# Attention of an attention-and-experts kernel, from eight batches of 128-token chunks to sixteen steps on 64x64 tiles

## The chip, the cores and the metric

The kernel runs on one core of one Trainium2 chip. The metric is the device time of one execution in microseconds (us), the median of three runs. A core has a matrix engine (PE, with its weight loads shown as PEld), three engines for elementwise work (DVE, ACT, POOL), and a queue engine SP that issues most DMAs. Matmuls read SBUF and write PSUM; both have 128 partitions.

## The reference, cut to what matters

```python
kv  = np.einsum('bhsd,bhse->bhde', k, v)      # b = 8 batches, h = 8 heads, s = 576, d = e = 64
out = np.einsum('bhsd,bhde->bhse', q, kv)
rms = np.sqrt(np.mean(out * out, axis=-1, keepdims=True) + 1e-06)
x   = (out / rms * g_norm)                    # then heads side by side: x[b, s, 512]
logits     = x @ w_gate                       # 8 experts
local_gate = sigmoid(x @ w_local)
# token by token in a batch: e = argmax(logits) if s == 0 or local_gate < 0.5,
# otherwise the expert of the token before
out[b, s] = softmax(logits)[e] * (relu(x @ w1[e]) @ w2[e])   # w1 512x1024, w2 1024x512
```

All arrays are float32.

## The kernel before, in words

The program has two parts. The first does the attention, the gate logits and the routing; the second runs the experts over tokens sorted by expert, with weights split into a high and a low half (`wsplit`) so that three fast matmuls stand for one of full precision.

**Attention.** The loop goes over the 8 batches. `load(b)` fetches k, v and q of one batch: of each head the first (or, for odd heads in k and v, the last) 512 tokens as four tokens to a partition on 128 partitions, and the 64 tokens that are left over two heads to a tile. `stage_kv` makes kv of all heads in the PSUM tile `pk`: 4 matmuls over 128 tokens and one over 64, for each head, two heads side by side on the columns of the array (L365). `stage_t` transposes kv and `stage_m` multiplies it by the gate weights, so that the logits come out of the same matmul as the output: the block matrix `kvb` holds kv and these gate columns. `stage_q` transposes q on PE into `pq`, and ACT copies it to `qT`. `out_two` then multiplies `qT` by `kvb`, two tokens and 146 columns at a time, on the whole array (L455), and `out_last` does the left-over tokens on 64x64 tiles (L471). ACT copies the result from `po` to `raw`. `squares` and a DVE sum give the mean square of each head, `rows_out` the normalisation and gate values, and `store` writes the rows of a batch to the DRAM array `xs`. After each pair of batches `route` works out, with a few matmuls into `rbank`, which expert each token takes and its place among that expert's tokens.

**Order.** The work of one batch is written down in pieces (`prepare`, `chunks`), and `step` puts pieces of `rows_out` and `route` between them with high priority. The order on PE, ACT, DVE and POOL in this part is then made by the planner of the language, from its own estimate of times. DMAs of SP run in the order in which they are written. k and v, and q, have two buffers of one batch each.

**Hand-over.** `begin` gathers the first two blocks of 128 tokens of expert 0 out of `xs`, splits that expert's weights, and turns the tokens; the first expert matmuls are in `first_wide` (written `ph`, L846). A third block follows when three quarters of the stores have landed, a fourth when all have. The rest of the second part has an order written by hand already and is the same in both kernels.

Of the kernel before, what the change touches and what calls it, by code (L numbers as in the profile page):

```python
# [22 lines left out]
def kernel(  # L23
# [22 lines left out]
    KS = 4  # L46
    PR = S - KS * P
    C = 2 * KS + 1
    KD = KS * D
# [3 lines left out]
    HB = 2 * PW  # L53
    KW = NG + HW + HB
    XO = NG
    NGRP = B // 2
    NCH = NGRP * C

# [11 lines left out]
    NM = NP * C // 2  # L70
# [54 lines left out]

    left = ctx.enter_context(ExitStack())
# [5 lines left out]
    lq = work.enter_context(tc.tile_pool(name="lq", bufs=2, reuse_waits="tile"))  # L132
# [10 lines left out]
    ld = right.enter_context(tc.tile_pool(name="ld", bufs=2, side="right", reuse_waits="tile"))  # L143
# [6 lines left out]
    ps_o = ps1.enter_context(tc.tile_pool(name="ps_o", bufs=4, space=PSUM,  # L150
# [71 lines left out]
    def heads(t):  # L222
        return t[:, 0:H * KD].rearrange("p (h c) -> p h c", h=H)

    def rest(t):
        return t[:, H * KD:].rearrange("p (n d) -> p n d", n=NP)

    def load(b):
        kt = ld.tile([P, H * KD + NP * D], F32, name="kt")
        vt = ld.tile([P, H * KD + NP * D], F32, name="vt")  # L230
        qt = lq.tile([P, H * KD + NP * D], F32, name="qt")
# [6 lines left out]
        kv = (k, kt), (v, vt)  # L238
        for src, dst in kv:
            main(dst, src, slice(0, H, 2), 0)  # L240
        for src, dst in kv:
            fetch(rest(dst), src[b].rearrange("(n x) s d -> n (x s) d", x=2)[
                :, KS * P:KS * P + P].rearrange("n p d -> p n d"))
        for src, dst in kv:
            main(dst, src, slice(1, H, 2), PR)
        if b >= 4:
            store(b - 4)
        main(qt, q, slice(0, H), 0)
        for y in range(2):
            fetch(rest(qt)[y * PR:(y + 1) * PR],  # L250
                  q[b, y * NP:(y + 1) * NP, KS * P:].rearrange("h p d -> p h d"))
        if b == B - 1:
            for i in range(NW1):
                wload(0, i)
        return kt, vt, qt

    loads = {b: load(b) for b in range(2)}
# [11 lines left out]


    FAR = 64
    cs = rc.tile([P, C], F32, name="cs")
# [3 lines left out]
    id1 = rc.tile([P, NGRP, C], F32, name="id1")  # L276

    def iota(dst, pattern, base, mult=0):
        nc.gpsimd.iota(dst, pattern=pattern, base=base, channel_multiplier=mult,
                       allow_small_or_imprecise_dtypes=True)  # L280

    for bb in range(2):
        js = slice(bb * (KS + 1), bb * (KS + 1) + KS)
        iota(cs[:, js], [[1, KS]], 2 * FAR * bb)
        iota(s8[:, js], [[E, KS]], 0, E * KS)
        iota(id1[:, :, js], [[2 * S, NGRP], [1, KS]], bb * S + 1, KS)
        nc.gpsimd.memset(m0[0:1, js.start:js.start + 1], 1.0)
        rows = slice(bb * PR, (bb + 1) * PR)
        iota(s8[rows, KS:KS + 1], [[E, 1]], E * KS * P, E)
        iota(id1[rows, :, KS:KS + 1], [[2 * S, NGRP], [1, 1]], bb * S + KS * P + 1, 1)  # L290
    nc.gpsimd.memset(cs[:, KS:KS + 1], float(FAR))
    m11 = rc.tile([P, C, C], F32, name="m11")
    csd = wk.tile([P, C, C], F32, name="csd", bufs=1)
    nc.vector.tensor_sub(csd, cs.unsqueeze(2).to_broadcast([P, C, C]),
# [58 lines left out]
    def stage_kv(b):  # L353
# [4 lines left out]
        if not b:  # L358
            order.sort(key=lambda x: x[2])
# [448 lines left out]
    for kvb in prepare(0):  # L808
        pass
# [419 lines left out]
```

## Time and profile before

| what | value |
|---|---|
| median of 3 runs | 620.85 us (619.88 to 621.93) |
| profiled execution | 623.8 us |
| its span, first to last instruction | 622.1 us |
| mean granted PE clock | 0.979 |
| PE, DVE, ACT, POOL busy | 588.8, 299.4, 232.9, 113.9 us |
| moved by DMA | 94.10 MB, 151 GB/s in the mean |
| first expert matmul | 140.18 us from the span's start |

A busy PE is not PE at its peak: matmuls are pipelined, and their records overlap. A row of a group gives its line, engine, operation, tiles (out<-in), shapes and count, then the union of its busy time in us, the mean duration of one in ns, and the engine's idle time just before them with what ended it. [...]

### The profile page before, as it was taken

The page shows a single profiled execution, that of the slowest core. Times are in us where ns is not written, and L with a number is a line of the kernel's source. Part 1 is how long each engine was busy: PE and PEld are TensorE (multiplying, and loading weights), DVE is VectorE, ACT ScalarE, POOL GpSimd, SP SyncE. Part 2 cuts the span into 40 slices and gives each one's busy share as a digit, 9 for nine tenths or more (in the row PEclk, how much of TensorE's full clock was granted, in tenths as well). Part 3 has the DMA queues.
Part 4 walks back from the last instruction along what each step waited for, and adds up shares of the span by engine and source line. Part 5 has one row for each costly group of instructions (what it writes and reads, how often), then busy time and mean ns, then how long its engine had stood idle before and what let it go on. Part 6 is the DMA issues. An engine that isn't in the chain of part 4 may idle for free. (4 is left out here: it accounts for less than half of the span.)

```text
span 622.1 us, 10287 instructions
## 1 busy us (share of the span) xinstructions
PE 588.8 (95%) x4069; PEld 519.3 (83%) x4069; DVE 299.4 (48%) x703; ACT 232.9 (37%) x392; POOL 113.9 (18%) x144
## 2 busy tenths in 40 slices
PE   5899998989897799999999999999999999999996
PEld 4788887878675798989897989899888979897895
DVE  2177988796736343615343436254525444362410
ACT  0266564484125323323333333234333333333310
POOL 5022313200152003011121120113020211201001
PEclk9999999878999799999999999999999999999999
DMA  9999999949376324323153323344342525231000
GB/s 249 278 310 301 299 259 280 307 164 279 124 245 215 107 77 140 103 101 116 68 174 103 109 82 110 136 119 139 103 141 79 174 98 154 75 114 58 1 35 23
DMA packets 63864, 94.10 MB, mean 151 GB/s; under 512 B 17471, under 2 KB 42047, under 8 KB 63808
## 3 DMA queue, kind: packets, MB, share of 16 engines
q1 hardware_dynamic: 56192, 72.31, 39.0%
q0 software_dynamic: 6304, 21.04, 10.9%
q8 instruction: 34, 0.56, 0.4%
q10 hardware_dynamic: 1312, 0.02, 0.1%
q14 instruction: 22, 0.18, 0.1%
HBM read 73.48 MB, written 20.53 MB: 151 GB/s over the span
## 5 line engine op out<-in xcount | busy, mean ns | idle before, releaser
L886 DVE SCALAR_TENSOR_TENSOR hl<-ph,hh 128x384 fp32r<-128x384 f32 (+3 forms) x92 | 53.4, 580 | 148.7 <-ACT hh L885 120.9
L880 POOL DMA_INDIRECT out_dram<-ot,sidr x36 | 35.4, 984 | 343.3 <-ACT ot L879 343.3
L885 ACT ACTIVATE hh<-ph 128x384 fp32r<-128x384 f32 (+3 forms) x92 | 46.9, 509 | 131.8 <-PE ph L852 126.4
L879 ACT ACTIVATE ot<-py,pe 128x512 f32<-128x512 f32 (+2 forms) x37 | 25.4, 687 | 111.7 <-issue 57.7
L365 PE MATMUL pk<-vt,kt 128*64 128x64 f32 (+1 forms) x640 | 42.7, 245 | 7.4 <-DMA vt<-in_v_dram 7.1
L365 PEld LDWEIGHTS pk<-vt,kt 128*64 128x64 f32 (+1 forms) x640 | 33.6, 146 | 16.9 <-issue 10.9
L744 POOL DMA_INDIRECT xr<-xs,gidr x36 | 37.8, 1051 | 24.7 <-DVE gs L1106 8.0
L455 PE MATMUL po<-kvb,qT 128*128 128x146 f32 x256 | 39.5, 300 | 0.0
L455 PEld LDWEIGHTS po<-kvb,qT 128*128 128x128 f32 x256 | 35.2, 198 | 0.8
L771 DVE SCALAR_TENSOR_TENSOR yl<-pt,gcol,yh 128x512 fp32r<-128x512 f32 x20 | 15.0, 751 | 37.0 <-ACT yh L770 36.8
L444 POOL TENSOR_TENSOR sq<-raw 128x512 f32<-128x512 f32 x17 | 17.7, 1044 | 74.1 <-ACT raw L457 38.6
L383 PE MATMUL pq<-ident,qt 128*128 128x128 f32 x128 | 24.1, 328 | 3.4 <-DVE kvb L415 2.8
L457 ACT COPY raw<-po 128x438 f32<-128x438 f32 (+1 forms) x48 | 22.5, 481 | 13.0 <-PE po L455 12.9
L385 ACT COPY qT<-pq 128x512 f32<-128x512 f32 x32 | 18.4, 585 | 19.4 <-PE pq L383 17.0
L445 DVE TENSOR_REDUCE ms<-sq 128x8 f32<-128x512 f32 x36 | 23.7, 680 | 3.6 <-ACT sq L442 2.7
L757 DVE TENSOR_TENSOR xr<-xr 128x512 f32<-128x512 f32 x37 | 25.3, 684 | 0.0
L846 PE MATMUL py<-w_1h,hh 128*128 128x512 f32 (+2 forms) x58 | 23.4, 403 | 0.0
L846 PE MATMUL py<-w_0h,hh 128*128 128x512 f32 (+2 forms) x58 | 23.3, 401 | 0.0
L766 PEld LDWEIGHTS pt<-ident,xr 128*128 128x128 f32 x148 | 18.3, 141 | 5.6 <-DVE xl L771 0.6
L852 PE MATMUL py<-w_0h,hl 128*128 128x512 f32 (+2 forms) x58 | 22.9, 394 | 0.1
L851 PE MATMUL py<-w_0l,hh 128*128 128x512 f32 (+2 forms) x58 | 22.8, 392 | 0.0
L852 PE MATMUL py<-w_1h,hl 128*128 128x512 f32 (+2 forms) x58 | 22.7, 392 | 0.0
(364 smaller groups left out, 1658.1 us busy)
## 6 DMA issues: line engine op xcount, KB each, us to landing
wst<-in_moe_w_dram SPq DMA_DIRECT2D x64, 512.0 KB
xs<-raw SPq DMA_DIRECT2D x8, 1132.0 KB
kt<-in_k_dram SPq DMA_DIRECT2D x16, 512.0 KB
vt<-in_v_dram SPq DMA_DIRECT2D x16, 512.0 KB
qt<-in_q_dram SPq DMA_DIRECT2D x8, 1024.0 KB
xs<-raw SPq DMA_DIRECT2D x8, 141.5 KB
kt<-in_k_dram SPq DMA_DIRECT2D x8, 128.0 KB
vt<-in_v_dram SPq DMA_DIRECT2D x8, 128.0 KB
```

Source lines behind the costliest of these rows:

```text
L365: nc.tensor.matmul(pk[bk * D:(bk + 1) * D, n, :], ks, vs, start=(c == 0), stop=(c == KS))
L383: nc.tensor.transpose(pq[:, w], heads(qt)[:, w // 2 * NP + n, w % 2 * P:w % 2 * P + P], ident)
L445: nc.vector.tensor_reduce(ms[:, j], sq.rearrange("p a (x d) -> p (a x) d", d=D), axis=AX.X, op=ALU.add)
L455: nc.tensor.matmul(po[:, h - h0], qT[:, h % NP, h // NP * 2 + w], kv_of(kvb, h), start=True, stop=True)
L744: i = nc.gpsimd.indirect_dma_start(out=xr[:, 0:XW], out_offset=None, in_=xs[0:rows], in_offset=bass.IndirectOffsetOnAxis(ap=idx, axis=0), ...
L757: i = nc.vector.tensor_mul(xv, xv, r.unsqueeze(3).to_broadcast([P, NP, 2, D]))
L846: mm = nc.tensor.matmul(ps, ah, bh, start=(first and i == 0), stop=False)
L852: nc.tensor.matmul(ps, al, bh, start=False, stop=(last and i == n - 1))
L879: nc.scalar.activation(ot[0:m], po[0:m], AF.Copy, scale=pe[0:m])
L880: nc.gpsimd.indirect_dma_start(out=outf, out_offset=bass.IndirectOffsetOnAxis(ap=idx[0:m], axis=0), in_=ot[0:m], in_offset=None, bounds_ch ...
L885: nc.scalar.activation(hh, ps, AF.Relu)
L886: nc.vector.scalar_tensor_tensor(hl, ps, 0.0, hh.bitcast(F32), op0=ALU.max, op1=ALU.subtract)
```

## The change

The attention is written anew. A step handles two heads of two batches, and there are 16 steps (4 pairs of batches times 4 pairs of heads). A batch's 576 tokens lie nine to a partition on 64 partitions, one batch on the lower 64 and the other on the upper 64, so there is no left-over chunk. Each load is one DMA for each batch, with 64 partitions and runs of nine tokens; three steps of k, v and q fit in the buffers (`LB`). All of kv (`kv`) and of the output (`q_kv`) runs on 64x64 tiles: kv on the two tiles of the diagonal, one for each batch, the output on all four, where the row half is the parity of the token and the column half the batch. `pk`, `po` and `kvb` are laid out to fit. The order of PE, ACT, DVE and POOL in the loop is written by hand (`manual_schedule`). Stores go out once for a pair of batches, and `rows_out` runs once for nine tokens in place of four and five. `route` has one product for the carry of the last choice in place of three.

```diff
-        def main(dst, src, hs, t0):
-            fetch(heads(dst)[:, hs], src[b, hs, t0:t0 + KS * P].rearrange("h (p c) d -> p h (c d)", c=KS))
...
+    def load(src, pool, nm, s):
+        g, n = divmod(s, NP)
+        t = pool.tile([P, 2, C * D], F32, name=nm)
+        for b in range(2):
+            fetch(t[b * D:(b + 1) * D],
+                  src[2 * g + b, 2 * n:2 * n + 2].rearrange("x (p c) d -> p x (c d)", c=C))
+        return t
...
+    def kv(s, x):
+        if not x:
+            pks[s] = ps_k.tile([P, 2, D], F32, name="pk")
+        kt, vt = kts[s], vts[s]
+        for c in range(C):
+            cd = slice(c * D, (c + 1) * D)
+            for b in range(2):
+                nc.tensor.matmul(pks[s][half(b), x], kt[half(b), x, cd], vt[half(b), x, cd],
+                                 start=(c == 0), stop=(c == C - 1))
...
+    def turn_kv(s):
+        pt = ps_q.tile([P, 3, P], F32, name="pt", tag="pq")
+        kvp = kvps.pop(s)
+        for t in range(2):
+            nc.tensor.transpose(pt[:, 0:2, half(t)], kvp, ident)
+        nc.tensor.transpose(pt[:, 2], qts[s].rearrange("p x f -> p (x f)")[:, 2 * W * P:C * P], ident)
+        kqs[s] = wk.tile([P, 3, P], F32, name="kq", bufs=3)
+        nc.scalar.copy(kqs[s], pt)
...
+    def q_kv(s):
...
+        for x in range(2):
+            po = ps_o.tile([P, 2, 512], F32, name="po")
+            cols = raws[g][:, :, n * PW + x * HW:n * PW + (x + 1) * HW]
+            for c in range(C):
+                w, r = divmod(x * C + c, 2)
+                lhsT = kq[:, 2] if w == 2 * W else qT[:, w // W, w % W]
+                o = (W if c == (0 if x else C - 1) else (c - x) // 2) * HW
+                for b in range(2):
+                    nc.tensor.matmul(po[half(b), r, o:o + HW], lhsT[half(r), half(b)],
+                                     kvb[half(r), b, x * HW:(x + 1) * HW], start=True, stop=True)
+            nc.scalar.copy(cols[:, x:x + 2 * W].rearrange("p (w r) e -> p r w e", r=2),
+                           po[:, :, 0:W * HW].rearrange("p r (w e) -> p r w e", e=HW))
+            nc.scalar.copy(cols[:, 0 if x else C - 1], po[:, x, W * HW:(W + 1) * HW])
...
+    STORES = {6: 0, 10: 1}
...
+    with tc.manual_schedule(engines=order):
+        for i in range(-2, NST):
+            new, nxt = i + 2 < NST, 0 <= i + 1 < NST
+            if new:
+                kv(i + 2, 0)
+            if i >= 0:
+                q_kv(i)
+            if new:
+                kv(i + 2, 1)
+                load_kv(i + 2 + LB)
...
+            if nxt:
+                logits_of(i + 1)
+            if new:
+                kvb_of(i + 2)
...
+            if nxt:
+                turn_q(i + 1, 0)
+            step()
+            if nxt:
+                turn_q(i + 1, 1)
+            if new:
+                turn_kv(i + 2)
+            if nxt:
+                load_q(i + 1 + LB)
+            if i >= 0:
+                sqs[i] = squares(i, i % 2 or i >= NST - 2)
+            step()
+            if i in STORES:
+                store(STORES[i])
+                if i == max(STORES):
+                    for j in range(NW1):
+                        wload(0, j)
```

Three places show what moves. In the rows stand the line, the operation and the tiles, the shape, and how many of that kind follow each other.

**SP, the end of the loads.** Before, the loads of batch 7 (k and v in six DMAs, a store, q in three), the weights of expert 0 and the next stores begin:

```order
L162 DMA kt<-in_k_dram 128x4x256
L162 DMA vt<-in_v_dram 128x4x256
L162 DMA kt<-in_k_dram 128x4x64
L162 DMA vt<-in_v_dram 128x4x64
L162 DMA kt<-in_k_dram 128x4x256
L162 DMA vt<-in_v_dram 128x4x256
L162 DMA xs<-raw 512x1x566
L162 DMA xs<-raw 64x566 x2
L162 DMA qt<-in_q_dram 128x8x256
L162 DMA qt<-in_q_dram 64x4x64 x2
L162 DMA wst<-in_moe_w_dram 128x1024 x4
```

After, the loads of the last steps, each in two DMAs of 64 partitions:

```order
L160 DMA kt<-in_k_dram 64x2x576 x2
L160 DMA vt<-in_v_dram 64x2x576 x2
L160 DMA qt<-in_q_dram 64x2x576 x2
L160 DMA xs<-raw 1152x1x566
L160 DMA wst<-in_moe_w_dram 128x1024 x4
L160 DMA qt<-in_q_dram 64x2x576 x2
L160 DMA wst<-in_moe_w_dram 128x2x512 x4
L160 DMA xs<-raw 1152x1x566 x2
```

The q of the last step now stands behind a store of two batches and the first four weight loads, and the small stores of 64 partitions are gone.

**PE, in the middle of the attention.** Before, a stretch of the planner's order (here the gate columns `pm` of one batch, the transposes of its q, and kv and output of its neighbours):

```order
L409 MATMUL pm<-gw,kvT 64x18 x8
L383 MATMUL pq<-ident,qt 128x128 x8
L365 MATMUL pk<-vt,kt 64x64 x13
L383 MATMUL pq<-ident,qt 128x128 x4
L365 MATMUL pk<-vt,kt 64x64 x7
L383 MATMUL pq<-ident,qt 128x128 x4
L365 MATMUL pk<-vt,kt 64x64 x11
L390 MATMUL pq<-ident,qt 64x128 x4
L365 MATMUL pk<-vt,kt 64x64 x8
L455 MATMUL po<-kvb_222,qT 128x146 x11
L397 MATMUL pt<-ident,kvp 128x128 x2
```

After, one whole step of the written order:

```order
L333 MATMUL pk<-vt,kt 64x64 x18
L392 MATMUL po<-kvb,qT 64x73 x32
L392 MATMUL po<-kvb,kq 64x73 x4
L333 MATMUL pk<-vt,kt 64x64 x18
L362 MATMUL pm<-gw,kq 128x18 x2
L374 MATMUL pq<-ident,qt 128x128 x8
L353 MATMUL pt<-ident,kvp 128x2x64 x2
L354 MATMUL pt<-ident,qt 128x128
```

The 64x64 work of a step now stands together, and the shape of the tiles changes twice a step.

**ACT, the end of the attention.** `w_0h` to `w_3h` are the casts of expert 0's weights. Before:

```order
L385 COPY qT<-pq 128x512
L210 CAST w_2h<-wst 128x1024
L391 COPY q_1904<-pq 64x512
L457 COPY raw<-po 128x2x219
L210 CAST w_3h<-wst 128x1024
L457 COPY raw<-po 128x2x219
L474 COPY raw<-po 128x292 x2
L457 COPY raw<-po 128x2x146
L442 ACTIVATE sq<-raw 128x512
L210 CAST w_0h<-wst 128x1024
```

After, from the squares of step 13 to those of step 14; the four casts here are those of the second weights:

```order
L422 ACTIVATE sq<-raw 128x1152
L208 CAST w_0h<-wst 128x1024
L208 CAST w_1h<-wst 128x1024
L394 COPY raw<-po 128x2x4x73
L396 COPY raw<-po 128x73
L208 CAST w_2h<-wst 128x1024
L208 CAST w_3h<-wst 128x1024
L394 COPY raw<-po 128x2x4x73
L396 COPY raw<-po 128x73
L375 COPY qT<-pq 128x512 x2
L422 ACTIVATE sq<-raw 128x1152
```

All four casts of the second weights now come ahead of the last copies of the attention; before, one of them did.

More of the change, by code (lines that the diff above doesn't have):

```diff
@@ L431, in steps, with squares @@
             step()
[L433 to L440 removed]
+    def squares(s, act):
+        g, n = divmod(s, NP)
+        if not n:
+            mss[g] = sm.tile([P, C, H], F32, name="ms")
+        x = raws[g][:, :, n * PW + XO:n * PW + XO + P]
+        sq = wk.tile([P, C, P], F32, name="sq", bufs=1)
         if act:
@@ L796, in begin @@
             wload(0, NW1 + i)
-        for b in range(4, 6):
-            store(b)
+        store(2)
         while len(ahead) < 3:
@@ L829 @@
+    sums(NST - 1, sqs.pop(NST - 1))
+    kk = sm.tile([P, C], F32, name="kk")
+    bg.append(rows_out(NGRP - 1, raws.pop(NGRP - 1), mss.pop(NGRP - 1), kk))
+    bg.append(route(NGRP - 1, kk))
     for _ in starting:
@@ L964 @@
         wsplit(0, NW1 + i, pin=False)
-    for b in range(6, 8):
-        store(b)
+    store(3)
     w = {i: wt[0, i] for i in range(NW1 + NW2)}
```

371 lines of the change are left out of this document (121 added, 250 removed).

## The prediction

> **What bounds the kernel now.** I read the page first: busy shares, the slices, the DMA issues. Then windows over the stages, the timeline of TensorE (PE) and of the DMA queue SP at the end of attention, and last the groups by line, for prices.
>
> The slices (each 15.55 us) show two kernels in one. For eight slices the DMA row stands at 9 and some 280 GB/s flow; from the tenth on DMA is light and PE full.
>
> ```profile
> PE 588.8 (95%) x4069; PEld 519.3 (83%) x4069; DVE 299.4 (48%) x703; ACT 232.9 (37%) x392; POOL 113.9 (18%) x144
> PE   5899998989897799999999999999999999999996
> PEclk9999999878999799999999999999999999999999
> DMA  9999999949376324323153323344342525231000
> GB/s 249 278 310 301 299 259 280 307 164 279 124 245 215 107 77 140 103 101 116 68 174 103 109 82 110 136 119 139 103 141 79 174 98 154 75 114 58 1 35 23
> ```
>
> The next rows are windows (length, busy time of PE, PEld, DVE, ACT, POOL with counts, granted clock, DMA share, GB/s): attention up to the first expert matmul, its middle, a stretch of loads alone, then the hand-over to the experts, and the experts.
>
> ```profile
> 0.00:140.20 140.20, 123.55 (x1418) 107.09 (x1418) 95.69 (x321) 70.39 (x150) 33.66 (x65) 0.95 0.98 272
> 22.00:113.00 91.00, 86.72 (x1076) 74.86 (x1075) 66.59 (x228) 49.99 (x111) 20.89 (x17) 0.97 1.08 294
> 35.00:55.00 20.00, 19.56 (x277) 16.31 (x276) 14.42 (x51) 11.93 (x27) 4.18 (x4) 1.00 1.13 306
> 140.20:206.30 66.10, 54.49 (x313) 44.42 (x313) 38.48 (x111) 21.82 (x34) 16.10 (x16) 0.95 0.67 213
> 206.30:622.00 415.70, 410.73 (x2340) 367.78 (x2340) 165.22 (x272) 140.69 (x209) 64.18 (x63) 0.99 0.32 101
> ```
>
> In 22 to 113 us the DMA share is above 1 while PE is busy 86.72 of 91 us: loading and PE are nearly balanced, and neither alone could be sped up by much. After 206.3 us PE is full and the change touches nothing there. So the change is worth what it does to the moment of the first expert matmul, 140.18 us in the rows of PE and SP below; all that follows (481.9 us of the span of 622.1) I carry over unchanged.
>
> ```profile
> 109.61 3.05 SPq L162 DMA_DIRECT2D qt<-in_q_dram  x3
> 112.70 25.56 SPq L162 DMA_DIRECT2D wst<-in_moe_w_dram  x8
> 136.33 1.04 PE L455 MATMUL po<-kvb,qT 128*128 128x146 f32 x7
> 137.20 1.04 PE L766 MATMUL pt<-ident,raw 128*128 128x128 f32 x8
> 140.18 0.62 PE L846 MATMUL ph<-raw,w_0h 128*128 128x256 f32 x3 [1.94 <-ACT raw L770]
> ```
>
> The last q load is issued at 109.6 and the first expert matmul starts 31 us later. The profiled execution took 623.8 us (span 622.1), 0.5% over the median of 620.85; I add the difference of spans to the median.
>
> **The bytes.** The DMA issues give them; they are the same after.
>
> ```profile
> wst<-in_moe_w_dram SPq DMA_DIRECT2D x64, 512.0 KB
> xs<-raw SPq DMA_DIRECT2D x8, 1132.0 KB
> kt<-in_k_dram SPq DMA_DIRECT2D x16, 512.0 KB
> vt<-in_v_dram SPq DMA_DIRECT2D x16, 512.0 KB
> qt<-in_q_dram SPq DMA_DIRECT2D x8, 1024.0 KB
> xs<-raw SPq DMA_DIRECT2D x8, 141.5 KB
> kt<-in_k_dram SPq DMA_DIRECT2D x8, 128.0 KB
> vt<-in_v_dram SPq DMA_DIRECT2D x8, 128.0 KB
> qt<-in_q_dram SPq DMA_DIRECT2D x16, 64.0 KB
> ```
>
> q, k and v are 27,648 KB, 28.3 MB. Half of the stores, 5094 KB or 5.2 MB, runs between the loads, before and after alike (batches 0 to 3; now as two stores of a group). Ahead of the last q load SP now also issues store 1 and four weight loads (2048 KB, 2.1 MB). So 35.6 MB must land before step 15 can be finished.
>
> **Loads: the term that decides.** Before, each big k, v or q load fills 128 partitions in runs of 1024 bytes, and the 64-token rests go in runs of 256. After, all 96 loads have runs of 2304 bytes and fill only 64 partitions, the lower half for one batch and then the upper for the other. Longer runs should help; half the partitions may hurt. The only 64-partition transfers with long runs before are the small xs stores: SP's last issues are one 128-partition store of batch 7, then two 64-partition ones. The windows below are: early loads in 1024-byte runs; weight loads; the 128-partition store; the two 64-partition ones; the worst and the best quarter microsecond among those.
>
> ```profile
> 3.00:6.00 3.00, 0.00 (x0) 0.00 (x0) 1.91 (x8) 0.36 (x1) 2.78 (x14) 1.00 1.05 338
> 120.00:125.00 5.00, 3.77 (x77) 3.16 (x77) 4.41 (x16) 1.40 (x4) 2.52 (x3) 0.99 1.02 361
> 163.00:164.00 1.00, 1.00 (x6) 0.79 (x5) 0.43 (x2) 0.25 (x1) 0.00 (x0) 1.00 1.03 383
> 164.80:165.80 1.00, 1.00 (x15) 0.82 (x14) 0.10 (x1) 0.00 (x0) 0.94 (x1) 1.00 1.04 276
> 165.00:165.25 0.25, 0.25 (x11) 0.25 (x10) 0.00 (x0) 0.00 (x0) 0.25 (x1) 1.00 1.01 199
> 165.50:165.75 0.25, 0.25 (x4) 0.25 (x3) 0.05 (x1) 0.00 (x0) 0.24 (x1) 1.00 0.99 362
> ```
>
> The DMA share stays at 1 while the rate falls from 383 to 276, and to 199 at worst: each packet takes longer. Sustained loads reach 306/338 = 0.905 of a clean stretch. That gives three prices for the loads: 383 x 0.905 = 347 GB/s if the half width costs nothing; 276 x 0.905 = 250 if it costs what these stores show; 199 if the worst stretch is the rule. I take 250, the row of the same transfer shape, though those are stores and not loads; 199 and 347 are the ends.
>
> Stores and weights keep 128 partitions (383 and 361 GB/s in clean stretches): 7.3 MB at 347 is 21 us. With the first issue at 2 us the last q load lands at T = 2 + 28.3/0.250 + 21 = 136 us (347: 105.6; 199: 165). It decides at T = 125: 28.3 MB in 102 us, or 277 GB/s.
>
> [...]
>
> **From the last load to the first expert matmul.** Of step 15 there remain the last transposes, q_kv(14), logits, turn_q(15) and q_kv(15). On ACT the order puts the four casts of expert 0's second weights among the copies of step 14, and those weights are loaded just behind the last q. Prices by group:
>
> ```profile
> L210 ACT CAST w_0h<-wst 128x1024 fp32r<-128x1024 f32 x4 | 4.2, 1040 | 0.0
> L457 ACT COPY raw<-po 128x438 f32<-128x438 f32 x32 | 16.5, 521 | 9.0 <-PE po L455 9.0
> L385 ACT COPY qT<-pq 128x512 f32<-128x512 f32 x32 | 18.4, 585 | 19.4 <-PE pq L383 17.0
> L442 ACT ACTIVATE sq<-raw 128x512 f32<-128x512 f32 x19 | 12.0, 639 | 5.8 <-DVE ms L445 5.5
> L770 ACT ACTIVATE xh<-pt,gcol 128x512 fp32r<-128x512 f32 x3 | 2.1, 688 | 3.3 <-PE pt L766 3.3
> ```
>
> Four weight loads at 347 GB/s take 6.0 us, the last cast then ends near T + 8. Behind it stand the raw copy of step 14 (584 and 73 columns, 0.9 us by the 438-column row), two qT copies (1.2), q_kv(15) on PE (1.4), its last raw copy (0.9), the squares of 1152 elements (1.2) and two xh (1.4): T + 15. First expert matmul at 151, 11 us later than 140.2, so 620.85 + 11 = 632. With 347 it is 121, hence 601; with 199 it is 180, hence 661.
>
> **What is moved under cover.** PE per step, from these pieces of the timeline (an f32 matmul is two records):
>
> ```profile
> 53.78 0.68 PE L365 MATMUL pk<-vt,kt 128*64 128x64 f32 x14
> 71.94 1.23 PE L471 MATMUL po<-kvb,q 64*64 64x73 f32 x28
> 65.44 1.09 PE L383 MATMUL pq<-ident,qt 128*128 128x128 f32 x8
> ```
>
> Less the tail of the last one (about 0.22, 0.23 and 0.33) they are 35, 37 and 109 ns apart. A step has 72 records of kv (2.5 us at the same 35 ns; in all the kv matmuls rise from 320 to 576, each over half the rows), 72 of q_kv (2.7 at 37 ns, where two column halves overlap; 1.3 if four tiles do), 11 transposes (1.2), and about 1.0 for logits, changes of tile shape and waits for two copies: 6.0 to 7.4 us. A step of loads takes 1.77/0.250 = 7.1 us, 8.0 with its share of store, so PE is covered; at 347 GB/s that cover is gone and PE sets the pace. ACT's copies come to about 4.5 us a step, DVE's squares' sums (1152 elements, 1.5 us by 680 ns for 512) to some 3, POOL's squares 2.4 every other step: all under 7. Removed zeroing of kvb, half the calls of rows_out, and two of route's three products lie under the same cover and bring nothing; neither did they stand on the path before, where DVE had 24 us free of 91. Loads wait for the kv two to three steps back, so SP holds two steps of work; q loads queue behind them, and store 1 with four weight loads stands ahead of the last q, which T counts.
>
> **Rivals.**
> 1. Forecast, 0.38: loads at 212 to 270 GB/s, T of 156 to 128, 652 to 624 us.
> 2. Lockstep, 0.12: all transfers keep to one half at a time from the first load on, as in the 199 row, 661 us. The row at 362 GB/s, half a microsecond later, speaks against it. It holds where the loads stay below 212 GB/s. [...]
> 3. Faster, 0.30: after one contended transfer the queues drift apart, some on the lower and some on the upper half, as the 362 row suggests, and a whole stream of alternating halves runs near full width. At 300 to 347 GB/s T is 117 to 106: 601 to 613 us. It decides above 277 GB/s. Against it: the pair of stores as a whole moved 276.
> 4. Faster but PE-bound, 0.12: loads as in 3, PE at 7.4 us a step. The first full step starts near 14 us, 13.9 steps later it is 117, plus 15 is 132: 613 us.
> 5. Loads near 277 GB/s, so nothing moves: 0.08.
>
> **How the numbers follow.** A change under 0.3% can't be told from none here (the runs spread by that much). Slower is 1 and 2, 0.50; faster 3 and 4, 0.42; same 0.08. The time is that of the likeliest, 632. The range 601 to 653 takes in 1, 3 and 4 and leaves out most of 2 and the rim of 3. The forecast's own range is 624 to 652.
>
> **What would show it.** Right: DMA share at 1 until about 136 us with 250 GB/s or a little more, SP's last q landing near there, PE idle for a quarter of each step waiting for kt, vt or qt, first expert matmul near 151, and the stretch behind it as long as before. By rival 3: GB/s above 300, first expert matmul near 120, PE waiting little. By rival 4: PE full and SP waiting for kv. If PE idles long, its granted clock may fall (the 7s and 8s in slices 8 to 10 and 14 of before, where gaps stand) and a cold PE, at twice 7 us, would become the bound itself: that would push past 652. If the experts' part also changes by more than 3 us, my carrying it over was wrong.

## The result, and the profile after

The changed kernel takes 688.44 us (median of 4 runs, 686.64 to 690.75), the kernel before 620.37 (620.85 in the three runs of the table above): a ratio of 1.1096, with a 95% interval of 1.1055 to 1.1137. It is 11% slower; 632 was forecast. The profiled execution took 688.0 us, span 686.3 (before: 623.8, span 622.1).

The page's busy row and four of its slice rows (one slice is 17.2 us):

```profile
PE 592.7 (86%) x5269; PEld 527.2 (77%) x5269; DVE 286.2 (42%) x587; ACT 239.8 (35%) x410; POOL 106.7 (16%) x125
PE   3757657772758995999999999999999999999997
PEclk9889868686558999999999999999999999999999
DMA  8999969887173645424232423525334244341000
GB/s 185 231 234 211 205 152 272 193 238 209 40 238 121 204 128 193 124 92 129 93 106 91 128 96 105 155 86 153 100 109 158 75 136 133 108 144 62 6 32 21
```

Before, eight slices ran with the DMA row at 9, some 280 GB/s and, after the first slice, PE at 8 or 9. Now the DMA row stands at 8 or 9 for five slices, with only 185 to 234 GB/s, and then swings between 9 and 1 while PE stays at 2 to 8: neither is full. PEclk stands below 9 in most of the first thirteen slices. From slice 14 on PE and its clock stand at 9, as before.

The same by stages (length, busy PE, PEld, DVE, ACT, POOL with counts, granted clock, DMA share, GB/s): up to the first expert matmul, its early part, its middle, the handover, the experts.

```profile
0.00:208.70 208.70, 128.11 (x2621) 114.51 (x2621) 87.24 (x218) 81.15 (x173) 27.42 (x47) 0.76 0.81 198
20.00:50.00 30.00, 21.47 (x493) 19.48 (x490) 4.29 (x13) 11.34 (x27) 2.11 (x1) 0.81 1.05 233
50.00:168.00 118.00, 76.74 (x1674) 69.09 (x1670) 49.28 (x126) 44.61 (x104) 18.04 (x9) 0.78 0.88 218
168.00:208.70 40.70, 22.69 (x353) 19.32 (x353) 30.98 (x65) 22.84 (x40) 3.14 (x2) 0.58 0.37 117
208.70:686.30 477.60, 464.55 (x2648) 412.65 (x2648) 198.92 (x370) 158.61 (x237) 79.31 (x78) 0.99 0.35 111
```

Up to the experts it took 208.7 us where it took 140.2: +68.5. The experts took 477.6 where they took 481.9: -4.3. The sum, 64.2, is the difference of the spans, so the whole loss lies in attention and the handover. Early on the DMA share is above 1 at 233 GB/s; in the middle the share is 0.88 and PE is busy 76.74 of 118 us at a clock of 0.78.

Rows of SP and PE: the last q issue, PE's first wait of the handover, the last one, the first expert matmul.

```profile
150.92 2.29 SPq L160 DMA_DIRECT2D qt<-in_q_dram  x2
169.25 1.11 PE L374 MATMUL pq<-ident,qt 128*128 128x128 f32 x4 [6.83 <-DVE kvb L363]
200.01 0.22 PE L570 MATMUL rbank<-oh,tri_b 128*128 128x72 bf16 x1 [8.42 <-DVE oh L562]
208.74 0.71 PE L789 MATMUL ph<-raw,w_0h 128*128 128x256 f32 x3 [2.05 <-ACT raw L683]
```

The last q is issued 41 us later than before (150.92 against 109.61); by the DMA packets the flow of loads ends at 167.6. From there to the first expert matmul it takes another 41 us. Waits of SP, PE and DVE (total, times, longest):

```profile
SPq L160 <- PE pm L362: 38.5, 8, 7.6
PE pk L333 <- issue: 16.0, 5, 4.8
PE pt L353 <- ACT qT L375: 9.5, 9, 2.2
DVE xa L670 <- DMA xa<-xs,gi: 15.4, 3, 14.8
```

SP, which should have had a full queue, waited 38.5 us for PE to give back k and v buffers. PE for its part waited for no k, v or q at all between 50 and 200 us. DVE stood 14.8 us in one piece for the gather of expert 0's tokens.

"Issue" in PE's waits means that nothing in the profile explains the wait. What does is the count of matmuls. PE's timeline from the end of one such wait to the end of the next:

```profile
44.75 1.01 PE L374 MATMUL pq<-ident,qt 128*128 128x128 f32 x4 [4.87 <-issue]
45.56 0.63 PE L353 MATMUL pt<-ident,kvp 128*128 128x128 f32 x2
45.98 0.42 PE L354 MATMUL pt<-ident,qt 128*128 128x128 f32 x1
46.33 2.07 PE L333 MATMUL pk<-vt,kt 64*64 64x64 f32 x33
48.10 0.38 PE L392 MATMUL po<-kvb,qT 64*64 64x73 f32 x1
48.10 0.31 PE L333 MATMUL pk<-vt,kt 64*64 64x64 f32 x1
48.10 0.38 PE L392 MATMUL po<-kvb,qT 64*64 64x73 f32 x1
48.20 0.32 PE L333 MATMUL pk<-vt,kt 64*64 64x64 f32 x2
48.28 1.34 PE L392 MATMUL po<-kvb,qT 64*64 64x73 f32 x60
49.45 0.22 PE L392 MATMUL po<-kvb,kq 64*64 64x73 f32 x1
49.45 0.23 PE L392 MATMUL po<-kvb,qT 64*64 64x73 f32 x2
49.45 0.35 PE L392 MATMUL po<-kvb,kq 64*64 64x73 f32 x7
49.64 0.51 PE L333 MATMUL pk<-vt,kt 64*64 64x64 f32 x12
53.71 0.91 PE L333 MATMUL pk<-vt,kt 64*64 64x64 f32 x24 [3.56 <-issue]
```

The counts ahead of the last row add up to 127. From PE's start, the longer waits without a releaser come after 345, 473, 600, 853, 1107, 1234, 1615, 1741 and 2249 matmul records: in steps of 127 or a multiple of it, give or take one, mostly in the middle of a k'v sum or of a group of transposes, where the data is there. Together these nine waits are 25.6 us. In the trace's DMA records, packets of 16384 bytes on the instruction queue start at 41.7 and 51.0 us, after PE had stopped at 39.9 and 50.2, take 1.2 to 1.3 us, and PE goes on 1.8 and 1.5 us after their end. All this says that PE is waiting for its program; e1 below tests it. The page counts a weight load for each matmul record (5269 of both), so 127 records are 254 instructions; over the whole span that queue brought 43 such packets, one for each 123 records. A step has 159 records here (two for each matmul, one for each transpose), 1.25 such pieces (2621 in all, with routing, up to the first expert matmul); before, the work of a step had 89 (1418 in all, divided by 16).

### The profile page after: what moved, and what is told of

It reads as the page before. It is cut to its first block, busy times and chain, and to the rows that moved or that the text cites. A ratio compares the mean times of both kernels' runs of the same rounds, so it can differ in the third digit from the quotient of the medians.

```text
span 686.3 us, 12576 instructions
## 1 busy us (share of the span) xinstructions
PE 592.7 (86%) x5269; PEld 527.2 (77%) x5269; DVE 286.2 (42%) x587; ACT 239.8 (35%) x410; POOL 106.7 (16%) x125
## 3 DMA queue, kind: packets, MB, share of 16 engines
q1 hardware_dynamic: 31808, 72.31, 38.5%
## 5 line engine op out<-in xcount | busy, mean ns | idle before, releaser
L333 PE MATMUL pk<-vt,kt 64*64 64x64 f32 x1152 | 56.3, 264 | 30.7 <-issue 16.0
L333 PEld LDWEIGHTS pk<-vt,kt 64*64 64x64 f32 x1152 | 51.5, 176 | 35.5 <-issue 35.1
L337 DVE COPY kvp<-pk 128x128 f32<-128x128 f32 x16 | 4.7, 291 | 83.4 <-PE pk L333 83.4
L424 POOL TENSOR_TENSOR sq<-raw 128x1152 f32<-128x1152 f32 x7 | 14.7, 2107 | 127.0 <-DVE ms L429 76.8
L392 PE MATMUL po<-kvb,qT 64*64 64x73 f32 x1024 | 29.4, 270 | 4.8 <-ACT qT L375 3.1
L392 PEld LDWEIGHTS po<-kvb,qT 64*64 64x64 f32 x1024 | 26.0, 171 | 6.1 <-ACT qT L375 3.4
L394 ACT COPY raw<-po 128x584 f32<-128x584 f32 x32 | 21.0, 656 | 23.8 <-PE po L392 23.7
L374 PEld LDWEIGHTS pq<-ident,qt 128*128 128x128 f32 x128 | 18.4, 178 | 14.0 <-DVE kvb L363 7.2
L344 ACT COPY kvb<-kvp 64x128 f32<-64x128 f32 x32 | 9.5, 298 | 50.5 <-DVE kvp L337 50.3
```

What stands on the lines that cost most here:

```text
L333: nc.tensor.matmul(pks[s][half(b), x], kt[half(b), x, cd], vt[half(b), x, cd], start=(c == 0), stop=(c == C - 1))
L374: nc.tensor.transpose(pq[:, w], qt[:, (x * W + w) * P:(x * W + w + 1) * P], ident)
L392: nc.tensor.matmul(po[half(b), r, o:o + HW], lhsT[half(r), half(b)], kvb[half(r), b, x * HW:(x + 1) * HW], start=True, stop=True)
```

## The experiments

The measure in all of them is the moment of the first expert matmul ("ph" below) in the profiled execution: 140.2 before, 208.7 after. The edits of e1 to e4, e13 and e18 change what is computed, and so the work of the experts; these ran once each, and only this moment is compared. The code below is cut to the lines that matter.

**No loads (e1).** After the first three steps, later steps use the same tiles.

```diff
-            kts[s] = load(k, ld, "kt", s)
+            kts[s] = load(k, ld, "kt", s) if s < LB else kts[s - LB]
```

> Leaves out all loads of q, k and v after the first three steps (the later steps compute on the data of the first three), so PE runs the same program with hardly any loads beside it. Read: the moment of the first expert matmul (208.7 us in the changed kernel, 140.2 before) and the gaps in PE. Theory C (code): PE stands still at the border of every 127 matmul records because the next 16 KB of its program come late, and they come late because they queue among saturated loads. Then the gaps shrink below 1 us, a step takes 6.5 to 7.5 us, and the first expert matmul comes near 135 us. Rival C2: a piece of program takes some 8.7 us by itself, loads or not: gaps stay, 20 pieces give 175 us or more. Rival L (loads alone set the pace, the gaps are something else that follows from late data): no gaps and 125 to 135 us, which C gives too; it is told from C by e3.

Its windows, and the row of ph (min, median and max ns; first and last start):

```profile
20.00:50.00 30.00, 26.58 (x722) 23.81 (x722) 9.63 (x23) 18.28 (x43) 4.21 (x2) 0.98 0.23 51
50.00:128.00 78.00, 57.33 (x1435) 51.72 (x1427) 44.90 (x116) 37.04 (x87) 15.94 (x8) 0.85 0.32 104
L789 PE MATMUL ph<-raw,w_0h x8: 278/283/415, 167.3 to 181.9; 128*128 128x256 f32 x8
```

No wait stands at a multiple of 127 any more, with the very same PE program. Between 27 and 51 us the packet of the next piece starts 0.1 to 1.2 us after PE enters a piece, where in the changed kernel those of 41.7 and 51.0 us started 5.6 and 6.3 us after. So in these two runs program pieces come late only beside saturated loads (DMA share 1.05 from 20 to 50 us, against 0.23 in e1; C right on this, C2 out). But ph is 167.3, not 135: without any load the changed attention is still 27 us behind the kernel before. All three theories had missed that; e13 to e18 go after it.

**128-partition loads (e2), fewer matmuls (e3), both (e4).**

```diff
-            fetch(t[b * D:(b + 1) * D],
-                  src[2 * g + b, 2 * n:2 * n + 2].rearrange("x (p c) d -> p x (c d)", c=C))
+            fetch(t[:, b],
+                  src[2 * g + b, 2 * n:2 * n + 2].rearrange("x (p c) d -> (x p) (c d)", c=C))
```

> Each load fills 128 partitions: two heads of one batch, where the changed kernel loads 64 partitions of two heads. Same bytes, same number of DMAs, same runs of 2304 bytes; the heads and batches then stand in other places, so the attention computed is another one. Theory L (half-width loads at 231 GB/s set the pace): the rate in 20 to 50 us rises from 231 to 300 or more GB/s, and the first expert matmul comes from 208.7 us to 165 or earlier. Theory C (PE waits for its program): the rate rises early on, but PE cannot follow; steps stay at 9 us or more, SP waits for PE, and the first expert matmul stays past 185.

```profile
20.00:50.00 30.00, 22.63 (x580) 20.37 (x578) 8.66 (x19) 15.59 (x36) 4.21 (x2) 0.94 0.79 278
50.00:140.00 90.00, 63.05 (x1420) 56.98 (x1411) 45.27 (x117) 36.86 (x87) 15.95 (x8) 0.78 0.76 244
L789 PE MATMUL ph<-raw,w_0h x8: 279/288/415, 179.2 to 194.2; 128*128 128x256 f32 x8
```

In 20 to 40 us the rate was 318 GB/s, with the share at 0.89, so loads no longer bound it; ph came 29.5 us earlier, between the two cases (165 and 185). The half width therefore costs some 29 us here, with what hangs on it, and 39 remain. Waits at program borders shrank (1.0, 2.1, 1.5 and 2.1 us up to 43 us) but did not vanish (4.7 us at 133.5).

e3 and e4 take out 72 of the 159 records of a step (one matmul for both batches; the same is done to q times kv):

```diff
-            for b in range(2):
-                nc.tensor.matmul(pks[s][half(b), x], kt[half(b), x, cd], vt[half(b), x, cd],
+            nc.tensor.matmul(pks[s][half(c % 2), x], kt[:, x, cd], vt[:, x, cd],
```

> Loads as in the changed kernel, but a step has 36 fewer matmuls (two records each): k'v adds up both batches in one matmul, and q times kv uses the first batch's kv for both. 87 records a step in place of 159, about as before the change. The attention is another one. Theory C: 127 records now last more than a step, the gaps at the borders go, and the loads at 231 GB/s set the pace: the last q lands near 146 us, first expert matmul 165 to 178. Theory L: with 231 GB/s as the only cause nothing changes, 200 to 209. A third, the order of routing steps: PE's waits of 4.3 us for oh stay; then 180 to 190.

> Both: 128-partition loads and 87 records a step. If code and loads are the two causes and add up, the rate is 300 GB/s or more, the last q lands before 125 us, and the first expert matmul comes at 125 to 150 us. If something else (the order of routing, the handover to the experts) holds the end, it stays past 160 though loads and PE are quick.

e3 reached ph at 201.2, e4 at 197.7. Waits at borders were gone in both, and yet only 7.5 and 11.0 us were gained; e4 is 18.5 us behind e2. e3 came out as theory L had it, e4 as its second case. The row of e4 says why:

```profile
20.00:40.00 20.00, 20.00 (x176) 18.10 (x176) 3.59 (x9) 8.75 (x19) 2.11 (x1) 1.00 0.76 259
L787 PE MATMUL ph<-raw,w_0h x8: 277/280/582, 197.7 to 212.2; 128*128 128x256 f32 x8
```

PE is busy all of 20 us with 176 records, where the changed kernel was busy 16.2 of the same 20 us with 366. Pairs of q times kv start 207 ns apart and transposes 213, against 109 for transposes in the kernel before: PE ran at half rate until 80 us, although busy without a gap from 12 to 67 us (the clock column shows 1.00 only because the trace holds no clock record before 82 us). In e3 transposes start 213 ns apart up to 36 us too, and its loads stay at 231 GB/s. So these two don't isolate the number of records: the shape of the matmuls changed as well, and PE ran at half rate meanwhile.

**Half-width loads in the kernel before (e9), and more records there (e8).**

```diff
-            fetch(heads(dst)[:, hs], src[b, hs, t0:t0 + KS * P].rearrange("h (p c) d -> p h (c d)", c=KS))
+            for y in range(2):
+                fetch(heads(dst)[y * PR:(y + 1) * PR, hs],
+                      src[b, hs, t0 + y * KS * PR:t0 + (y + 1) * KS * PR].rearrange(
+                          "h (p c) d -> p h (c d)", c=KS))
```

> The kernel before, with every big k, v and q load (1024-byte runs) split into two DMAs of 64 partitions, lower half and upper half one behind the other; same bytes, same packets. Theory L (a transfer into half of the partitions runs slower, and two on opposite halves don't mend it): the rate in 35 to 55 us falls from 306 to 230 to 250 GB/s, the last q lands 20 to 30 us later and the first expert matmul comes at 158 to 172 us, 638 to 655 in all. If what is slow in the changed kernel is something else (the 2304-byte runs): 300 GB/s and no change.

```profile
35.00:55.00 20.00, 13.13 (x178) 11.22 (x176) 7.43 (x30) 5.31 (x13) 1.04 (x1) 0.83 1.16 215
L849 PE MATMUL ph<-raw,w_0h x8: 274/280/415, 164.7 to 179.2; 128*128 128x256 f32 x8
```

306 GB/s became 215, ph moved by 24.5 us, and the time to 652.17 (ratio 1.053, 1.0488 to 1.0572), 31.5 us more; the profiled execution, with 646.63, was the quickest of four. The computation and the data packets are the same. There are twice as many of these DMAs, each of half the size, so this run alone doesn't part width from size; e2 does, where the number and the size of the DMAs stayed and the rate rose with the width (233 to 278 GB/s from 20 to 50 us). The rate falls below the 230 to 250 expected, between the 250 of the prediction and its row of 199.

e8, the kernel before with its q times kv matmuls in four:

```diff
-                nc.tensor.matmul(po[:, h - h0], qT[:, h % NP, h // NP * 2 + w], kv_of(kvb, h),
+                for e0 in range(0, PW, 37):
+                    nc.tensor.matmul(po[:, h - h0, e0:min(e0 + 37, PW)], qT[:, h % NP, h // NP * 2 + w],
+                                     kv_of(kvb, h)[:, e0:min(e0 + 37, PW)],
```

> The kernel before, with each q times kv matmul of 146 columns written as four of 37, 37, 37 and 35: the same loads, the same columns through PE, 768 more records in attention (1418 to 2186, or 17 pieces of program where 11 were). Theory C (a piece that must come within the time of 127 records, beside saturated loads, stalls PE): gaps of 1 to 4 us appear at multiples of 127 records, PE's clock falls behind them, and the first expert matmul comes 5 to 25 us later than 140.2. If only the columns count and pieces come early enough: within 3 us of 140.

e8 took 780.89 to 803.49 us in five executions, over a quarter more than the 620.67 of the kernel before beside it, with ph at 302.2: both cases missed. There was not one wait at a program border, so pieces came early enough. But the matmuls of 37 columns were not cheaper:

```profile
L456 PE MATMUL po<-kvb,qT 128*128 128x37 f32 x1018 | 194.2, 370 | 0.0
40.00:60.00 20.00, 20.00 (x122) 19.21 (x122) 4.24 (x14) 4.73 (x10) 2.08 (x2) 0.50 0.27 74
```

1018 records took 194.2 us of PE where 256 took 39.5 before: each loads its 128x128 weights again (122 loads beside 122 records in the second row), and the clock was at half for long. Two in a row start 112 ns apart at full clock, against 124 for the 146 columns before. The second row is a window of 20 us: PE is busy throughout, on 128x128 weights, and the clock is at half. As a test of program pieces it failed, since PE was slowed more than its program grew.

**Waits in the changed kernel one by one (e5, e6, e11, e12).** e5 puts one more step between the ranks and the choice of the expert in route (and one less at its end); e6 scales both gathered tiles of expert 0 in program order; e11 besides keeps the split of w2 behind the first matmuls; e12 fills the waits for oh with 32 idle matmuls.

```diff
         yield                             # e5, in route
+        if g < NGRP - 1:
+            yield
         ca = sm.tile([P, 1], F32, name="ca")
-            scale(xrs[x], False)          # e6, in begin
+            scale(xrs[x], True)           # both ahead of the turns
-        wsplit(0, NW1 + i, pin=False)     # e11
+        wsplit(0, NW1 + i, pin=True)
+        for _ in range(32):               # e12, ahead of L570
+            nc.tensor.matmul(rbank[:, 256:384], ones_b, ones_b, start=True, stop=True)
```

> The changed kernel, with one more yield in route between the ranks (pb, pre) and the choice of the expert (ca to oh), so that PE comes to the count matmuls of L570 after its transposes, one step place later. In the changed kernel PE waits there 4.34 + 4.33 + 8.42 us for oh, while DVE does the sums. Theory R (these waits are on the path, and the half clock that follows them too): the waits fall to below 2 us each, the first expert matmul comes 8 to 18 us earlier (191 to 200 us), the time falls from 688 to 670 to 680. Theory C+L (late program pieces and half-width loads set the pace): what PE saves here it waits a step later for its program or its data; 0 to 4 us.

> The changed kernel, with the two scalings of expert 0's gathered tokens (xa) kept in program order on DVE, so that they stand behind the copies of the last two steps and not ahead of those of step 14. In the changed kernel DVE stands there 14.8 us for the gather, and PE 6.83 us behind it (kvb). If that stall is on the path, the first expert matmul comes 5 to 12 us earlier (197 to 204), 676 to 683 us in all. If the end is held by the chain of routing and weight casts anyhow: less than 3 us.

> e6 and besides the splits of expert 0's second weights (w2) kept behind its first matmuls in program order, so that they no longer stand on DVE between the pieces of route(2) at 180 to 198 us. PE waited there 7.9 to 8.4 us for oh. If that chain holds the first expert matmul, it comes 5 to 9 us before e6's 198.6; what of it stays in the time depends on whether the second matmuls then wait for w2: 669 to 677. If the chain is held elsewhere: no change from e6 (677).

> The changed kernel with 32 bf16 matmuls of no use (128 columns of ones) on PE just ahead of each group of L570 matmuls, where PE waits 4.3, 4.3 and 8.4 us for oh. They take some 2 us at full clock of time that is waited anyway. If the half clock behind such waits (10.2, 6.8 and 20.5 us at half rate) is due to PE standing still, part of it goes and the first expert matmul comes 3 to 10 us earlier (199 to 206). If not, no change or 1 to 3 us later.

e6 is as expected: DVE's 14.8 us are gone, the time is 677.21 (1.0915, 1.087 to 1.0961), 11 us less.

```profile
L790 PE MATMUL ph<-raw,w_0h x8: 277/297/415, 198.6 to 213.0; 128*128 128x256 f32 x8
```

e11 has ph at 192.0, 6.6 us before e6, and the time is 676.66, the same: what the first matmuls gain, the second ones wait for w2. e5 shortened the waits for oh (4.3 to 2.3 and 3.1), but PE then waited 11.3 us for ab from POOL; 685.56, with ph at 201.6 in the quickest of its four executions. e12 took 686.83, ph at 205.9, the rim of its first case. In time both gain under 3 us, and their intervals (1.1025 to 1.1108 and 1.1004 to 1.1121) overlap with that of the changed kernel: when one of these waits shrinks, the next takes its place.

**What remains without loads (e7, e10, e13 to e18).** e7 is a full version with 128-partition loads and e6's edit. e10 drops the order written by hand, e17 does so on e7, e18 on e1. e13 is e1's counterpart of the kernel before. e14 gives the small tiles four PSUM buffers and takes one of the two of po, e15 moves routing as e5 and off POOL, e16 does both; all three on e7.

```diff
-    with tc.manual_schedule(engines=order):     # e10, e17, e18
+    with ExitStack():
-        by_hand.append(True)
-    ps_q = ps1.enter_context(tc.tile_pool(name="ps_q", bufs=2, space=PSUM,      # e14
+    ps_q = ps1.enter_context(tc.tile_pool(name="ps_q", bufs=4, space=PSUM,
-    ps_o = ps1.enter_context(tc.tile_pool(name="ps_o", bufs=2, space=PSUM,
+    ps_o = ps1.enter_context(tc.tile_pool(name="ps_o", bufs=1, space=PSUM,
-            return (nc.vector if g >= NGRP - 2 else nc.gpsimd).tensor_mul(      # e15
+            return nc.vector.tensor_mul(
-                nc.tensor.matmul(pks[s][half(b), x], kt[half(b), x, cd], vt[half(b), x, cd],   # e7
+                nc.tensor.matmul(pk[half(b)], kt[half(x), b, cd], vt[half(x), b, cd],
-                    nc.tensor.matmul(po[half(b), r, o:o + HW], lhsT[half(r), half(b)],
+                    nc.tensor.matmul(po[half(b), (c - x) % 2, o:o + HW], lhsT[half(r), half(x)],
```

> The changed kernel's computation with 128-partition loads, written out in full: a half of the partitions holds a head in place of a batch, k'v and q times kv take their rows from there, k'v of the two heads of a step goes through PSUM one after the other; and the two scalings of xa pinned as in e6. If half-width loads (29.5 us between the changed kernel and e2) and the stall for the gather (10 us in e6) are separate causes, the first expert matmul comes at 169 to 175 us and the time is 648 to 655. If the wide loads had already hidden the stall, 177 to 181 and 656 to 661. Nobody's theory gives less than 160: without loads at all it was 167.

e7: 661.24 us (1.0662, 1.0618 to 1.0707), ph 180.15: the quick loads had already hidden the gather, as the second case said. So the 29.5 us of e2 and the 10 of e6 are in part the same time.

> The kernel before, leaving out all loads of q, k and v after its first two batches (later batches compute on their data); the counterpart of e1, in which the changed kernel without loads reached the first expert matmul at 167.3 us. Theory P (beside loads and program pieces, the changed kernel's engines need longer for the same attention): without loads the kernel before is bound by PE alone, 86.72 of 91 us busy, and reaches it at 120 to 135 us, so 32 to 47 us ahead of e1. If it comes at 100 or earlier, PE was never near its limit before and my reading of a balance was wrong. If at 140, the loads never bounded it.

```profile
20.00:50.00 30.00, 28.91 (x372) 25.30 (x373) 12.49 (x50) 14.05 (x30) 4.13 (x4) 1.00 0.32 105
50.00:100.00 50.00, 49.96 (x616) 42.30 (x614) 43.46 (x144) 27.81 (x65) 11.03 (x9) 1.00 0.28 96
L856 PE MATMUL ph<-raw,w_0h x8: 276/278/383, 135.3 to 148.0; 128*128 128x256 f32 x8
```

The kernel before is bound by PE: without loads PE is busy 49.96 of 50 us at full clock, and ph gains only 5 us. The changed one in its middle (e1 above) has 57.33 of 78 us at 0.85. Where its time goes can be seen in e1's waits, and in its rows of `pm`, one for each step:

```profile
PE rbank L570 <- DVE oh L562: 16.1, 3, 7.4
PE pt L353 <- ACT qT L375: 11.3, 13, 2.4
PE po L392 <- ACT qT L375: 5.4, 3, 2.2
46.49 0.62 PE L362 MATMUL pm<-gw,kq 128*128 128x18 f32 x4
52.19 0.62 PE L362 MATMUL pm<-gw,kq 128*128 128x18 f32 x4
63.17 0.62 PE L362 MATMUL pm<-gw,kq 128*128 128x18 f32 x4
```

Up to 52.2 us four steps take 5.6 to 5.7 us each. There `rows_out` and `route` begin to run beside the steps, and from then to 119 us every second step takes 11 to 12 us, with two waits for qT or one for oh in it. In e1 PE waited 32.8 us for qT and oh, in e13 3.8 for qT and none for oh.

> e7 (180.15 us to the first expert matmul, 661 in all) with four PSUM buffers for the small tiles pm, pq, pt (two before) and one for po (two before). A step now turns over four small tiles where the kernel before turned seven over in the work of four steps. If the waits for their copies (qT, 17.7 us in e7) hold the path, they fall below 5 us, and the first expert matmul comes 6 to 14 us earlier (166 to 174); the one po buffer gives back 1 us a step at most. If something else is late just behind (DVE's sums, the casts), 0 to 4 us. Worse than e7 if po binds: 182 to 196.

> e7 with the yield of e5 in route and its mask product (ids, 2.65 us on POOL for the first two groups) on DVE. In e5 the wait for oh became one for ab from POOL (11.3 us). If the chain of routing holds the path, PE's waits for oh and ab (16.6 us in e7) fall below 8 us and the first expert matmul comes 5 to 12 us earlier (168 to 175). If the gaps only move to the next wait, 0 to 3 us.

> e7 with the edits of e14 and e15 together. If both waits are on the path and separate, their gains add up: 156 to 168 us to the first expert matmul, 637 to 649 in all. If either alone had opened the same slack, no better than the better of the two. None of the theories lets it beat the kernel before (140.2): the last two steps with the casts of the weights take 44 us in e7, 13 of which are PE work.

e14 took 683.55 us, the case "worse if po binds", with ph at 206.2 beyond the range given for it: waits for qT did not go (17.2 us, now ahead of po), and sixteen new ones for po came. e15 took 660.94, equal to e7. e16, both, took 694.76, worse than either. One window of e14:

```profile
77.00:107.00 30.00, 24.36 (x350) 22.46 (x351) 12.71 (x32) 9.17 (x21) 4.79 (x2) 0.50 0.64 211
```

PE is busy 24.36 of 30 us and yet at half clock throughout; in it stand two of e14's new gaps ahead of po, 0.88 and 0.87 us, and one of 3.88 for oh. The clock did not change in this window, and with the wait for oh in it the window can't show whether the short gaps alone would hold it at half.

> The changed kernel without the order written by hand: the scheduler orders PE, ACT, DVE and POOL by its own simulated times, as it did before the change; it slips single k'v matmuls between the transposes, the route matmuls and the copies they wait for. Loads and SP's order by the same rules. Theory O (the order written by hand leaves PE waiting for oh, qT, kvb and the gather, and the half clock after each wait doubles it): these waits go, the half-width loads at 231 GB/s set the pace, the last q lands near 146 to 150, first expert matmul 163 to 178, time 643 to 658. Theory C (program pieces late beside saturated loads whatever the order): gaps at multiples of 127 records stay, 190 or more, over 670. In both the handover may keep some of its 26 us.

> e7 (128-partition loads, scalings of xa pinned) with the order left to the scheduler, as in e10. In e10 the scheduler's order took as long as the one written by hand, but beside half-width loads. If the order by hand costs time once the loads are quick, the first expert matmul comes 8 to 25 us before e7's 180 (155 to 172; 636 to 653 in all). If the tiling itself (four small tiles and twice the records a step) makes the waits whatever the order, it stays at 174 to 186 (655 to 667).

> e1 (all loads of q, k and v after the first three steps left out) with the order left to the scheduler. e1 took 167.3 us to the first expert matmul, the kernel before without loads 135.3. If the order by hand is what those 32 us are, this comes at 135 to 150. If it is the tiling and the small steps, 158 to 172.

e10 took 689.39 (ph 207.8), e17 677.19, e18 reached ph at 192.9, none better than the same kernel in the order by hand (688.44; 661.24; ph 167.3). The order by hand is not the cause as against the planner's; beside quick loads it is the better one. e10's time fits theory C's case, but its waits without a releaser were down to 3.8 us: PE waited for kvb, kvp and oh instead. A window of e17, and ph:

```profile
140.00:160.00 20.00, 19.46 (x295) 17.17 (x295) 12.05 (x42) 7.63 (x18) 4.69 (x3) 0.50 0.99 328
L788 PE MATMUL ph<-raw,w_0h x8: 280/283/415, 193.5 to 209.9; 128*128 128x256 f32 x8
```

PE is busy 19.46 of 20 us, at half clock.

## Why the prediction was wrong, step by step

**What held.** The bytes; that loads of half width cost time, the largest single cost found (29.5 of 68.5 us); that early on the DMA share stays at 1 while the rate falls (1.05 at 233 GB/s). The part behind the first expert matmul came 4.3 us shorter than carried over, which is over the 3 us that the prediction had set as a sign against this step. At 347 GB/s the sum for T gives 104.6 and not 105.6, which moves the lower end of the range by 1 us and nothing else.

**Loads, T.** The term was mis-sized: 250 GB/s was taken, 233 came (20 to 50 us), and 215 in e9. With 28.3/0.233 = 121 and 23 for the rest, T would have been 144 and not 136: 8 us. I trusted the mean of two stores (276) more than the stretch in which the worst stood.

**"PE is covered".** This is the step that failed. I priced a step of PE at 6.0 to 7.4 us and set it against 7.1 to 8.0 us of loads. From 54.6 to 160.5 us ten steps took 10.6 us each, by the starts of `pm`. SP waited 38.5 us for k and v buffers while PE waited for no load, and the last load landed at 167.6, 23 us past the 144 that the loads need. The matmuls themselves were priced about right: undisturbed steps of e1 took 5.6 to 5.7 us. I had summed matmuls at full clock and left out what stands between them: program pieces (16 us of issue waits on k'v alone), copies of small tiles (qT, 9.5), oh (8.7 up to 200 us), and the clock, 0.78 from 50 to 168 us. That the clock may fall when PE idles stood in the text as a danger that would push past 652, but in none of the rivals and with no chance.

**The tail, T + 15.** It took 41 us. DVE first stood for the gather (two scalings ahead of step 14's copies, e6: 10 us), then did the split of w2 between the pieces of routing (8.4 us of wait for oh, e11), and all of it at a clock of 0.58. I had read ACT's order there and not DVE's. The second weights were also not loaded just behind the last q, as the sum has it with T + 8. SP issued them 34 us after it, when DVE split the first weights and so gave back the four staging buffers `wst`:

```profile
183.89 1.21 DVE L209 TENSOR_TENSOR w_0l<-wst,w_0h 128x1024 fp32r<-128x1024 f32 x1
185.13 4.12 SPq L160 DMA_DIRECT2D wst<-in_moe_w_dram  x4
```

Together: 8 + 23 + 26 = 57 us, which, up to rounding, is 208.7 less the 151 forecast.

**The rivals.** Lockstep (661) had the right direction and gave 27 us too little; half width put into the kernel before makes 652 (e9). The two faster rivals needed 277 GB/s and more; e2 reached that only with full width (278). Rival 4, PE-bound at 7.4 us a step, was right that PE takes over, but beside slow loads and not quick ones, and at 10.6 us a step.

**Where the 68.5 us went.** 29.5 for half-width loads (e2), with the wait for the gather that slow loads bring (e6 and e7); 12 more that go when there are no loads at all, program pieces among them (179.2 to 167.3); 27 that stay without loads (32 if the kernel before is also taken without loads, e13). In these 27 stand PE's waits for qT and oh, which come with `rows_out` and `route` beside small steps, and the clock (0.85 in e1 from 50 to 128 us). The planner's order (e10, e17, e18) and routing off POOL (e15) did not win them back. More PSUM buffers were not tested alone, since e14 took one from po. Why the clock stays low is open. Gaps alone don't explain it: in e17 and e8 PE is busy 19.46 and 20.00 of 20 us at a clock of 0.50. The 64x64 tiles alone don't either: in e1 they run from 20 to 50 us at 0.98, and e8's half clock is on 128x128 weights. e2 computes another attention and e1 repeats its data, so these three shares are good to a few us.

## What to carry to other kernels

Fill 128 partitions with each load: 28.3 MB took some 25 to 32 us longer in halves (e2, e9). Count instructions as well as columns: 127 matmul records were one 16 KB piece of program, and where PE ran through a piece in less than 7 to 9 us beside saturated loads, it waited for the next. When an engine is said to be covered, price its waits and its clock too, not only its work, and read the new order on every engine at the handover.

## What the runs showed of the hardware

- Program pieces: PE entered a piece at 36.1 and 44.8 us, the packets for the next started 5.6 and 6.3 us later, and PE went on another 3.0 and 2.7 us later; at the nine borders with a wait, a piece became usable 7.2 to 9.0 us after PE had entered the one before. Without loads (e1) the same program never waited at a border.
- Clock: it stayed at half for 20 us in which PE was busy 19.46 (e17), for 20 us in which it was busy all the time on 128x128 weights (e8), and for 55 us without a gap (e4, by the spacing of matmuls). So a busy PE row says little about the clock.
- A matmul of 37 columns on 128x128 float32 weights cost nearly as much as one of 146: starts 112 against 124 ns apart at full clock, 213 against 245 at half (e8 and the kernel before).
